# Output rows of a fused scan and feed-forward kernel placed in buffers that an earlier phase has left

## Chip, cores, metric

One Trainium2 chip, one core. The metric is the device time of one execution in microseconds; lower is better. A version is timed in rounds beside the kernel before on the same chip.

In the lines of the profile PE is TensorE, DVE VectorE, ACT ScalarE, POOL GpSimd, and SPq the queue of SyncE (SP), from which most transfers are issued. A line gives start and duration in microseconds, the engine, the line of the kernel (L622), output and inputs; `x3` means three instructions merged. A bracket at the end is the idle time before and what the profile thinks ended it. "Granted clock" is the share of TensorE's full clock that it got; a half-clock window is a stretch at 0.50.

## The reference, cut to what matters

```python
B, H, S, D = 4, 8, 768, 48
for t in range(S):                      # complex decay a_n, |a_n| <= 0.999
    S_re, S_im = a_n[t] * (S_re, S_im)  # complex product
    S_re += outer(k[t], v[t])
    y[t] = q[t] @ S_re
x = y.transpose(0, 2, 1, 3).reshape(3072, 384)
ffn = (gelu(x @ w_gate) * (x @ w_val)) @ w_out
out = x + sigmoid(x @ w_res) * ffn      # (3072, 384) fp32
```

The scan is done in 12 chunks of 256 steps (`g`), grouped in units `u`: [0], [1,2], [3,4], [5,6], [7,8], [9,10], [11]. In one phase the kernel finishes the attention part of unit `u`, prepares the decays of unit `u+1` and writes the output rows of unit `u-1`. So "the third phase" writes the rows of unit 1 (`op_step(1, 0..3)`), and 128 tokens are one output row block, called a row here. The gelu stretch of a phase is where PE computes `gp` and `vp` (`x @ w_gate`, `x @ w_val`) and ACT the gelu.

## The kernel before: what the change and the argument touch

```python
sqp = ctx.enter_context(tc.tile_pool(name="sqp", bufs=2))   # has the tags "qk" and "atm"
ob  = ctx.enter_context(tc.tile_pool(name="ob", bufs=2))    # the output rows
...
TURN = 3            # chunks g < 3: q and k are turned by TensorE and copied to "qk";
                    # chunks g >= 3: turned by DMA transposes (QT, KT)
...
# attention, chunks 1 and 2 only
qk = sqp.tile([128, 1024], BF, tag="qk", name="qk")
nc.scalar.copy(out=qk[0:DD, 0:512], in_=tp[0:DD, 0:512])
nc.vector.tensor_copy(out=qk[0:DD, 512:1024], in_=tp[0:DD, 512:1024])
...
def op_step(u, jj):
    h2 = T["h2", u]
    ps = psM.tile([128, DM], FP, tag="mm", padded_shape=[128, 512], name="op")
    for ffi in range(KF):
        nc.tensor.matmul(out=ps, lhsT=h2[:, ffi, jj * 128:(jj + 1) * 128], rhs=wo[:, ffi, :],
                         start=(ffi == 0), stop=(ffi == KF - 1))
    ot = ob.tile([128, DM], FP, tag="ot", name="ot")
    nc.vector.scalar_tensor_tensor(out=ot, in0=T["sg", u][:, jj], scalar=1.0, in1=ps, op0=OP.add, op1=OP.mult)
    t0 = (CHUNK[UNITS[u][0] + jj // C] * C + jj % C) * 128
    ...
    nc.sync.dma_start(out=out[t0:t0 + 128, :], in_=ot)
...
# in the same queue (SP): loads of q, k, a_re, a_im, and the transposes
T["turn"] = nc.sync.dma_start_transpose(out=tt, in_=pads[nm, g % 2])
...
# second gelu stretch: one chunk's loads go between the two chunks' transposes
if u == 1:
    steps[4:4] = [call(late, "turn", call(load_a, g)) for g in range(8, 9)]
```

Tiles of one tag share the pool's buffers in turn; a tile that gets a buffer waits for whatever last read it. For an output row that is the store of the row that had the buffer before.

## Time and profile before

| | before |
|---|---|
| median of 3 runs (range) | 289.26 us (288.54 to 289.46) |
| the profiled run | 291.91 us, span 290.1 |
| PE, DVE, ACT busy | 84%, 74%, 68% |
| DMA queue of SP | 67.7% of 16 engines |
| waits of a row for a store | 1 of 24, 2.97 us |

The profile is of a run 2.7 us longer than the median, though it still counts as fast. The lines of the profile that count are shown in the prediction.

### The profile page before, as it was taken

The page shows a single profiled execution, that of the slowest core. Times are in us where ns is not written, and L with a number is a line of the kernel's source. Part 1 is how long each engine was busy: PE and PEld are TensorE (multiplying, and loading weights), DVE is VectorE, ACT ScalarE, POOL GpSimd, SP SyncE. Part 2 cuts the span into 40 slices and gives each one's busy share as a digit, 9 for nine tenths or more (in the row PEclk, how much of TensorE's full clock was granted, in tenths as well). Part 3 has the DMA queues.
Part 4 walks back from the last instruction along what each step waited for, and adds up shares of the span by engine and source line. Part 5 has one row for each costly group of instructions (what it writes and reads, how often), then busy time and mean ns, then how long its engine had stood idle before and what let it go on. Part 6 is the DMA issues. An engine that isn't in the chain of part 4 may idle for free.

```text
span 290.1 us, 5128 instructions
## 1 busy us (share of the span) xinstructions
PE 244.3 (84%) x1834; PEld 146.3 (50%) x1848; DVE 214.6 (74%) x376; ACT 198.6 (68%) x336; POOL 93.3 (32%) x141
## 2 busy tenths in 40 slices
PE   0444958979789979979699999989999998999994
PEld 0122536855444545534356554556545665456782
DVE  0679996993999667878396998869977677564553
ACT  4877997688894799855479975778565646455250
POOL 4021841130245405465304393124911242100220
PEclk9999768997999999999799999999999999999998
DMA  8999999899999999959999979999599566910631
GB/s 147 187 174 187 170 199 198 145 188 201 158 206 200 171 203 178 176 127 139 185 209 165 131 114 186 207 174 79 74 213 205 104 56 129 185 23 21 144 54 55
DMA packets 176001, 44.01 MB, mean 152 GB/s; under 512 B 165092, under 2 KB 175976, under 8 KB 175976
## 3 DMA queue, kind: packets, MB, share of 16 engines
q1 hardware_dynamic: 140744, 33.05, 67.7%
q0 software_dynamic: 35232, 10.64, 35.7%
q8 instruction: 14, 0.23, 0.3%
q14 instruction: 11, 0.09, 0.1%
HBM read 31.33 MB, written 9.08 MB: 139 GB/s over the span
## 4 chain that ended last, share of the span: by engine, by line
PE 60%; ACT 14%; DVE 10%; DMA 9%; issue 4%; SPq 2%; DVEq 0%; ACTq 0%
PE vp L599 14%; PE gp L595 13%; PE op L619 11%; PE csl L272 6%; DMA KT<-padK 3%; ACT L639 3%; PE cst L291 3%; PE rp L611 3%; DMA ar<-in_a_re_dram 3%; PE at L446 2%; ACT CS L144 2%; SPq L172 2%; PE dk L488 1%; DMA k<-in_k_dram 1%; ACT ar L144 1%
## 5 line engine op out<-in xcount | busy, mean ns | idle before, releaser
L144 ACT ACTIVATE h<-gp 128x512 bf16<-128x512 f32 (+1 forms) x84 | 44.5, 535 | 41.5 <-PE gp L595 41.2
L602 DVE SCALAR_TENSOR_TENSOR h<-h,vp 128x512 bf16<-128x512 bf16 (+1 forms) x84 | 50.3, 606 | 20.6 <-PE vp L599 13.3
L595 PE MATMUL gp<-xT,wg 128*128 128x512 bf16 (+1 forms) x238 | 61.2, 352 | 4.4 <-DVE xT L586 2.0
L599 PE MATMUL vp<-xT,wv 128*128 128x512 bf16 (+1 forms) x252 | 62.3, 354 | 0.9 <-ACT xT L584 0.8
L619 PE MATMUL op<-wo,h 128*128 128x384 bf16 x288 | 50.7, 326 | 1.3 <-ACT xT L584 1.3
L599 PEld LDWEIGHTS <-wv 128*128 128x128 bf16 x252 | 24.9, 99 | 23.9 <-issue 2.2
L619 PEld LDWEIGHTS <-h 128*128 128x128 bf16 x288 | 27.3, 98 | 18.5 <-issue 2.3
L634 POOL DMA_DIRECT2D out_dram<-x x22 | 19.9, 953 | 46.5 <-DMA out_dram<-ot 45.1
L595 PEld LDWEIGHTS <-wg 128*128 128x128 bf16 x252 | 23.7, 99 | 21.3 <-issue 4.5
L316 POOL DMA_DIRECT2D m<-d x32 | 22.5, 709 | 36.4 <-DMA d<-Ei 15.4
L449 DVE TENSOR_TENSOR atm<-at,mask 128x512 bf16<-128x512 f32 x36 | 24.6, 683 | 9.0 <-PE at L446 9.0
L639 ACT ACT_TABLE_LOAD x21 | 26.9, 1283 | 1.1 <-PEq L844 0.7
L178 POOL DMA_DIRECT2D v<-in_v_dram x24 | 21.6, 906 | 17.6 <-DMA ai<-in_a_im_dram 12.3
L201 POOL COPY landed<-k 1x1 f32<-1x1 f32 x9 | 2.7, 296 | 65.2 <-DMA k<-in_k_dram 65.2
L272 PE MATMUL csl<-lm,lt0a 128*128 128x384 f32 x24 | 12.1, 589 | 11.6 <-ACT lm L144 11.6
L622 DVE SCALAR_TENSOR_TENSOR ot<-sg,op 128x384 f32<-128x384 f32 x24 | 13.1, 547 | 11.4 <-PE op L619 6.9
L446 PE MATMUL at<-QT,KT 96*128 96x128 bf16 x144 | 14.4, 220 | 4.5 <-DMA KT<-padK 4.0
L291 PE MATMUL cst<-ai,ut0b 128*128 128x384 f32 x40 | 17.3, 523 | 0.6 <-DVE ot L622 0.4
L144 ACT ACTIVATE CS<-ai,hpi 128x768 bf16<-128x768 f32 x12 | 11.2, 935 | 8.7 <-DVE ai L301 8.7
L144 ACT ACTIVATE ar<-ar 128x768 f32<-128x768 f32 x20 | 16.9, 853 | 0.1
L501 ACT CAST x<-y 128x384 bf16<-128x384 f32 x22 | 10.5, 477 | 9.3 <-PE y L498 8.8
L235 DVE CUSTOM_DVE_ANT_0 lm<-lm,sq 128x768 f32<-128x768 f32 x12 | 11.4, 949 | 7.3 <-ACT sq L231 7.3
(113 smaller groups left out, 458.2 us busy)
## 6 DMA issues: line engine op xcount, KB each, us to landing
ar<-in_a_re_dram SPq DMA_DIRECT2D x24, 192.0 KB, 5.6
ai<-in_a_im_dram SPq DMA_DIRECT2D x24, 192.0 KB, 4.4
q<-in_q_dram SPq DMA_DIRECT2D x24, 192.0 KB, 4.1
k<-in_k_dram SPq DMA_DIRECT2D x24, 192.0 KB, 5.1
out_dram<-ot SPq DMA_DIRECT2D x24, 192.0 KB, 2.8
out_dram<-x POOLq DMA_DIRECT2D x22, 192.0 KB, 4.8
v<-in_v_dram POOLq DMA_DIRECT2D x24, 96.0 KB, 5.0
wg<-in_moe_w_gate_dram POOLq DMA_DIRECT2D x4, 288.0 KB, 7.7
```

Of the source, the lines that this page charges most:

```text
L144: return tab(nc.scalar.activation(**kw))
L178: held(nc.gpsimd.dma_start(out=t[:, c], in_=rows(v, g, c)), after)
L272: nc.tensor.matmul(out=cs, lhsT=lmat[c], rhs=T["lm", g][:, sl], start=True, stop=True)
L291: nc.tensor.matmul(out=cs, lhsT=tmat[c if s == 0 else 1], rhs=th[:, sl], start=True, stop=(s == 0 or c == 0))
L316: T["turned"] = nc.gpsimd.dma_start(out=m[u * D:(u + 1) * D].rearrange("p r h -> p (r h)"), in_=md.rearrange("r (h d) -> d (r h)", h=H))
L446: nc.tensor.matmul(out=at[:, j], lhsT=T["KT", g][0:DD, x0 + j], rhs=T["QT", g][0:DD, x0 + j], start=True, stop=True)
L449: nc.vector.tensor_tensor(out=atm, in0=at, in1=mask4, op=OP.mult)
L595: nc.tensor.matmul(out=gp, lhsT=wg[:, fi, ffi * 128:(ffi + 1) * 128], rhs=xT[:, fi, :], start=(fi == 0), stop=(fi == KD - 1))
L599: nc.tensor.matmul(out=vp, lhsT=wv[:, fi, ffi * 128:(ffi + 1) * 128], rhs=xT[:, fi, :], start=(fi == 0), stop=(fi == KD - 1))
L602: T["gmul"] = nc.vector.scalar_tensor_tensor(out=h2[:, ffi, :], in0=h2[:, ffi, :], scalar=0.5, in1=vp, op0=OP.mult, op1=OP.mult)
L619: nc.tensor.matmul(out=ps, lhsT=h2[:, ffi, jj * 128:(jj + 1) * 128], rhs=wo[:, ffi, :], start=(ffi == 0), stop=(ffi == KF - 1))
L639: tab(nc.scalar.preload_act_table_set(nm))
```

## The change

Its intent: give the output rows more buffers without more memory. After chunk 2 the two `qk` buffers are never used again, so rows with odd number, from the third phase on, go there.

```diff
-        ot = ob.tile([128, DM], FP, tag="ot", name="ot")
+        if u > 0 and jj % 2:
+            ot = sqp.tile([128, 1024], BF, tag="qk", name="ot2").bitcast(FP)[:, 0:DM]
+        else:
+            ot = ob.tile([128, DM], FP, tag="ot", name="ot")
```

## The prediction

> **What bounds the kernel now.** I read the page first, then the waits of the whole run and those of VectorE (DVE) alone, then the chain that ended last, then timelines of the stretch that the waits pointed to, and last that stretch's DMA share.
>
> The page says that no engine is full on average: PE 84%, DVE 74%, ACT 68%. The chain says what sets the end after the first half: from 150 us on it is nearly all matmuls, and between 150 and 264 us PE is busy 110.2 of 114 us (the windows view). So time saved before 150 us arrives at the end unless DMA holds it up; store waits after 150 us would have to show in the waits view first.
>
> The change can only act where an output row `ot` waits for a buffer. DVE's waits, longest first in total (us in total, times, longest), show one such wait:
>
> ```profile
> DVE h L602 <- PE vp L599: 13.3, 27, 0.7
> DVE atm L449 <- PE at L446: 9.0, 8, 2.5
> ...
> DVE ot L622 <- DMA out_dram<-ot: 3.0, 1, 3.0
> ```
>
> One of the 24 rows waits for a store to land, for 3.0 us. A second view agrees: of the 20 separate semaphore instructions that the sequencer runs ahead of the `ot` line, the median takes 21 ns and the longest 2095 ns. The DVE timeline shows where (start, duration, what, [idle before]):
>
> ```profile
> 117.83 0.54 DVE L622 SCALAR_TENSOR_TENSOR ot<-sg,op 128x384 f32<-128x384 f32 x1
> ...
> 121.62 0.55 DVE L296 TENSOR_TENSOR lm<-cst,lm 128x384 f32<-128x384 f32 x1
> 125.14 0.55 DVE L622 SCALAR_TENSOR_TENSOR ot<-sg,op 128x384 f32<-128x384 f32 x1 [2.97 <-DMA out_dram<-ot]
> 125.61 0.55 DVE L301 TENSOR_SCALAR ai<-lm 128x768 int32<-128x768 int32 x1
> 126.08 0.35 DVE L586 COPY xT<-tpx 128x384 bf16<-128x384 bf16 x1
> 126.35 0.94 DVE L381 TENSOR_TENSOR padQ<-CS,q 128x1536 bf16<-128x1536 bf16 x1
> ```
>
> This is the third row of the third phase. The first row was computed at 113.17; its store left eight microseconds later, because the sync queue (SP) was still issuing loads:
>
> ```profile
> 118.45 3.04 SPq L164 DMA_DIRECT2D ai<-in_a_im_dram  x2
> 121.59 4.47 SPq L626 DMA_DIRECT2D out_dram<-ot  x3
> 127.36 3.22 SPq L385 DMA_TRANSPOSE QT<-padQ  x1
> 130.67 0.53 SPq L626 DMA_DIRECT2D out_dram<-ot  x1
> 131.25 3.83 SPq L385 DMA_TRANSPOSE KT<-padK  x1
> ```
>
> The chain that ended last goes through this very wait (start, us, what):
>
> ```profile
> 121.59 3.46 DMA out_dram<-ot
> ...
> 125.14 0.55 DVE ot L622
> 125.70 0.48 DVE ai L301
> 126.18 0.02 issue
> 126.20 1.67 ACT CS L144 x2
> 127.87 0.02 issue
> 127.89 1.28 ACT L639
> ...
> 131.25 10.00 DMA KT<-padK
> ```
>
> So the reader should see a store issued late, not a slow store, and a DVE that stands in order behind it with ready work (`ai`, `xT`, `padQ`).
>
> **What the Trainium skill says.** (1) "TensorE: Matmul & The Clock Gate", section "Architectural detail", calls ACT and DVE strict FIFO. The trace agrees: L301 had its input at 122.17 and started at 125.61, after `ot`. (2) "Perfetto Trace Analysis", section "DMA Instruction — HWDGE", says that the queue's row starts when its semaphores are satisfied and leaves out the data movement. The trace agrees: the store's row starts at 121.59 and DVE is released at 125.05, 3.46 us on. (3) "DMA: Bandwidth & Descriptors", section "Issuing engines are not separate DMA queues": all DMAs share 16 engines. It matters for whether transposes moved forward would meet loads; see below. (4) The clock-gate page, section "What's actually happening": the clock falls to half after an idle window of about 3.4 us, the window running freely. The trace has such a fall: after PE's wait for `KT` the granted clock was 0.50 in 142 to 144 us and 0.77 in 144 to 146.
>
> **The change, part by part.** It adds and removes no instruction. Rows with odd number, in the third and later output phases, take the `qk` buffers: 4+4+4+4+4+2 = 22 rows lie there, so 11 move and 13 stay. A row is 384 fp32 = 1536 bytes per partition and the `qk` buffer 2048, so it fits and costs no memory. The `ot` instruction stays 128x384 fp32 from PSUM, 0.55 us. The last matmul reading `qk` started at 72.7 us (view of that tile); the first row put there belongs at about 117.8, so the new buffers bring no wait of their own.
>
> In the third phase rows 0 to 3 now have four buffers: row 2 takes the one last used by the second phase's second row, stored long ago. Its other inputs: the matmuls of row 2 start at 119.50 and last 2.11, end 121.61; DVE is free at 122.17. So row 2 starts near 122.17 and not 125.14: **2.97 us**, all of that idle stretch.
>
> Does it reach the end? Step by step after it:
> - DVE: L301 at 122.6, `xT` at 123.1 (its transpose ends 122.93), `padQ` at 123.4, done 124.3, `padK` 125.2. Row 3 follows at about 125.1; its matmuls started 122.77 and end 124.88, just in time. Full 2.97 kept.
> - ACT: idle 3.66 us before `CS` for L301. It starts 2.97 earlier, as do the table load (127.89 to 124.9) and the first gelu (129.18 to 126.2).
> - PE: its first `gp` waits 1.60 us for `xT`. That wait goes; PE is then free at 124.9, gains 1.6, fills its four PSUM buffers, and waits for the gelu. From the gelu on (129.83 resumption becomes 126.9) it is 2.97 earlier, so the end of `rp` moves from 138.73 to 135.8.
> - SP: loads end at 121.5 as before; the third store leaves near 123, `QT` at 124.4 instead of 127.36, row 3's store after it, `KT` at 128.3 instead of 131.25. With 3.83 of issue and 6.17 to landing, as now, `KT` lands at 138.3 instead of 141.25.
> - So PE's wait for `KT` stays 2.56 us, between 135.8 and 138.3, and everything behind it is PE work shifted by 2.97.
>
> Is there room in DMA? The windows view, one us each (last two columns: share of 16 engines, GB/s), says yes:
>
> ```profile
> 124.00:125.00 1.00, 0.89 (x6) 0.40 (x5) 0.00 (x0) 0.00 (x0) 0.98 (x3) 1.00 0.83 219
> 125.00:126.00 1.00, 0.00 (x0) 0.00 (x0) 0.86 (x2) 0.00 (x0) 0.00 (x0) 1.00 0.22 33
> ...
> 128.00:129.00 1.00, 0.91 (x5) 0.38 (x4) 1.00 (x3) 1.00 (x1) 1.00 (x2) 1.00 0.00 0
> ```
>
> The loads have drained by 125; the engines then stand nearly empty until the transposes start. A `QT` issued at 124.4 meets only the last of the loads; I charge an estimated 0.2 us for it (a third of the 0.6 us between 124.4 and 125). Sum: 289.26 - 2.97 + 0.2 = **286.5 us**.
>
> Later phases: no other row waits for a store, and their rows 0 and 2 lie 6 to 9 us apart with the first store issued within 0.6 us (the fourth phase: row 0 at 159.18, store 159.75, row 2 at 167.70). Gain there: nil.
>
> **Rivals.**
> - *The wait is replaced.* If `KT` comes no earlier, because the transposes are paced by the loads before them, PE waits for it longer and nothing is gained: about 289. For it: `KT` already makes PE wait 2.56 us, and the second unit's `QT` issue took 6.51 us, so transposes do queue up. Against: the DMA share of 0.00 at 128 to 129. I give it one in ten, and half-way cases (287.5 to 288.5) the same.
> - *The clock.* The shift moves PE's idle stretch against the freely running clock window. The present fall costs, as an estimate from the granted clocks, 2 x (0.12 + 0.50 + 0.23) = 1.7 us. If the new run escapes it, 285; if it meets a second one, 288. Neither has evidence; one in eight each.
> - *The order changes.* Buffer availability could enter how the instruction streams are put in order. Against: in the third, fourth and fifth phases alike DVE runs the last L296, row 2, then L301, though only the third phase has the wait; the order does not look shaped by it. If it changes anyway, either direction by up to 2%.
> - *The wait was hidden anyway.* Then 289. Against: DVE, ACT (3.66) and PE (1.60) idle together there.
>
> **Range and chances.** The three runs before spread 0.9 us. Full gain, 286.3 to 286.7, is the likeliest; a partly lost gain stretches the range up more than a lucky clock stretches it down: 285.3 to 288.3. Over 2% faster means below 283.5, twice the one wait there is; only a new order or clock could do that: 4%. Over 2% slower: 3%. Within: 93%.
>
> **What would show it right or wrong.** Right: no DVE wait for `out_dram<-ot`; row 2 near 122.2 and L301 right behind it; `QT` issue at 124.4 and `KT` landing near 138.3; the stretch after it the same as before but about 2.8 to 3.0 us earlier; `ot` still 0.55 us. Wrong: PE's wait for `KT` grows from 2.56 towards 5; or the granted clock differs at 138 to 146; or DVE's sequence differs; or the wait reappears at another row.

## The result

| | before | changed |
|---|---|---|
| median (range), same rounds | 288.9 us (287.73 to 289.46, 4 runs) | 285.74 us (284.71 to 289.11, 4 runs) |
| ratio | | 0.9884, interval 0.9834 to 0.9934 |
| profiled span | 290.1 | 282.9 |

A ratio here is the mean time of one kernel's fast runs over that of the other's fast runs in the same rounds, so it is not quite the ratio of the medians. One of the four runs of the changed kernel (289.11) counts as slow and is left out of it. Executions over 1.5% slower than the fastest of the same kernel are left out of the means. The predicted 286.5 lies 0.8 us from the median.

The order of the instructions on every engine was compared: it is the same in both kernels. So no gain comes from a new order; what can differ is where rows lie, how long instructions wait, and what follows.

The DVE timeline of the changed kernel (L625 is the row, L622 before), the counterpart of the stretch shown in the prediction:

```profile
117.67 0.55 DVE L625 SCALAR_TENSOR_TENSOR ot<-sg,op 128x384 f32<-128x384 f32 x1
...
121.46 0.55 DVE L296 TENSOR_TENSOR lm<-cst,lm 128x384 f32<-128x384 f32 x1
121.93 0.54 DVE L625 SCALAR_TENSOR_TENSOR ot<-sg,op 128x384 f32<-128x384 f32 x1
122.39 0.55 DVE L301 TENSOR_SCALAR ai<-lm 128x768 int32<-128x768 int32 x1
122.86 0.35 DVE L586 COPY xT<-tpx 128x384 bf16<-128x384 bf16 x1
123.12 0.95 DVE L381 TENSOR_TENSOR padQ<-CS,q 128x1536 bf16<-128x1536 bf16 x1
```

There is no bracket behind row 2 any more, and the row takes the same 0.54 us. The queue of SP in the changed kernel:

```profile
117.07 3.24 SPq L164 DMA_DIRECT2D ai<-in_a_im_dram  x2
120.41 2.42 SPq L629 DMA_DIRECT2D out_dram<-ot  x3
124.14 1.80 SPq L385 DMA_TRANSPOSE QT<-padQ  x1
126.03 1.08 SPq L629 DMA_DIRECT2D out_dram<-ot  x1
127.16 3.98 SPq L385 DMA_TRANSPOSE KT<-padK  x1
```

The stores still leave only when the loads are out (120.41), 7 us after row 0 was computed. What changed is that nobody waits for them. `QT` leaves 3.2 us earlier than before.

The spans of the two profiles differ by 7.2 us, more than twice what the times differ by. Two things lie behind that, both in the stretch after row 2. PE's waits between 126 and 150 us, before and then changed:

```profile
PE at L446 <- DMA KT<-padK: 2.6, 1, 2.6
PE gp L595 <- DVE xT L586: 1.6, 1, 1.6
```

```profile
PE dk L488 <- DVE Gb L411: 0.2, 1, 0.2
```

The wait for `KT`, which I had expected to stay, is gone. And so is the half-clock window that followed it. The windows view (after the busy times: clock granted, DMA share, GB/s), before, cut at the clock's own steps, and then changed:

```profile
138.09:141.50 3.41, 0.85 (x8) 0.40 (x7) 1.32 (x6) 2.27 (x5) 2.05 (x3) 1.00 1.36 199
141.50:144.91 3.41, 3.19 (x19) 1.81 (x18) 1.15 (x2) 0.60 (x1) 0.00 (x0) 0.50 1.32 178
```

```profile
137.00:146.00 9.00, 8.92 (x98) 5.58 (x98) 8.29 (x15) 7.22 (x15) 0.64 (x1) 1.00 1.33 204
```

The clock did not simply get better, though. The changed profile has a half-clock window of its own in the second phase, from 104.98 to 108.39 us, which the one before lacks. Of the later profiles below, all nine of edited or changed kernels that are of use have it there too, and not behind `KT`; the useful one of the kernel before (rerun_before2) again has it only behind `KT`. Row 0 of the third phase came at 112.5 to 114.6 us with the earlier window (turn_first, with another order of loads, apart) and at 113.2 and 113.6 without it.

One profile each cannot tell which of this belongs to the change and which to the run. The experiments had to.

### The profile page after: what moved, and what is told of

It is laid out like the page before. It is cut to its first block, busy times and chain, and to the rows that moved or that the text cites. A ratio compares the mean times of both kernels' runs of the same rounds, so it can differ in the third digit from the quotient of the medians.

```text
span 282.9 us, 5119 instructions
## 1 busy us (share of the span) xinstructions
PE 242.6 (86%) x1834; PEld 145.9 (52%) x1848; DVE 215.1 (76%) x376; ACT 198.8 (70%) x336; POOL 93.8 (33%) x141
## 4 chain that ended last, share of the span: by engine, by line
PE 66%; ACT 11%; DMA 7%; SPq 6%; issue 4%; DVE 3%; POOL 2%; ACTq 0%; DVEq 0%; POOLq 0%
PE op L619 14%; PE vp L599 14%; PE gp L595 14%; PE csl L272 6%; SPq L164 4%; PE cst L291 3%; PE rp L611 3%; PE at L446 2%; DMA ar<-in_a_re_dram 2%; ACT L642 2%; DMA d<-lm 2%; PE dk L488 2%; PE cst L293 2%; PE tpx L580 2%; DMA k<-in_k_dram 2%
## 5 line engine op out<-in xcount | busy, mean ns | idle before, releaser
L637 POOL DMA_DIRECT2D out_dram<-x x22 | 20.7, 988 | 42.0 <-DMA out_dram<-ot 37.5
L625 DVE SCALAR_TENSOR_TENSOR ot<-sg,op 128x384 f32<-128x384 f32 x24 | 13.2, 549 | 8.6 <-PE op L619 5.6
L501 ACT CAST x<-y 128x384 bf16<-128x384 f32 x22 | 10.5, 477 | 8.8 <-PE y L498 8.5
L144 ACT ACTIVATE sg<-rp 128x384 f32<-128x384 f32 x24 | 11.6, 491 | 6.5 <-PE rp L611 5.4
```

The costliest lines, as they stand in the source:

```text
L144: return tab(nc.scalar.activation(**kw))
L637: nc.gpsimd.dma_start(out=out[t0:t0 + 128, :], in_=x, accum_op=OP.add)
```

## The experiments

Theory: one wait, row 2 of the third phase for row 0's store, is all that the change removes, and its 3 us reach the end. Rivals: the later phases' buffers carry some of it; it is chance; the buffers' place and not their number matters; the store is slow, not late. Twelve kernels ran, four on one chip each. Single runs scatter more on these chips than the first three did: the kernel before ranged from 286.2 to 292.7 within one call.

### Is it chance? Both kernels again

No edit to either. rerun_before:

> The kernel before, unchanged, against itself. If the gain of the change is real and not drawn by chance: ratio 1.000 within 0.004. If run-to-run scatter alone makes 1% (rival), the ratio can be as far off as 0.99. Its second profile: DVE waits again 2 to 4 us for the store of row 0 at row 2 of the third phase; PE waits for KT about 2.6 us after that if this wait belongs to the kernel, anything from 0 to 3 us if it is a matter of the run.

rerun_after:

> The changed kernel again, for a second profile. My theory (one wait of 3.0 us removed and carried to the end): ratio 0.988 to 0.991, no DVE wait for a store in the third phase, and if my step on KT was right PE waits about 2.6 us for KT in the third gelu stretch; the first profile of the changed kernel showed no such wait. If it is absent again, the moved transposes land sooner than I reckoned, and the gain in the profile is above 3 us.

Measured (ratio to the kernel before, interval): rerun_before 1.0003 (0.9942 to 1.0063); rerun_after 0.9919 (0.9866 to 0.9972). The profiled run of rerun_before took 637 us, with PE busy for 602 of them, and says nothing about the kernel. The profile of rerun_after has neither the wait at row 2 nor a `KT` wait behind it. Later, on a third chip, both once more. rerun_before2:

> The kernel before against itself again, because its last profile was of a run of 635 us and is no use. Ratio 0.997 to 1.003. Profile: the wait of 2 to 3.5 us at row 2 of the third phase, and 1.5 to 3 us of PE wait for KT behind it, with a half-clock window after it if PE's wait is over 2 us.

rerun_after2:

> The changed kernel beside third_only3 on the same chip, to settle whether the third phase alone carries the gain. My theory: 0.988 to 0.993 and within 0.004 of third_only3. Profile: no store wait at row 2, a PE wait for KT behind it of 0 to 1.3 us, not the 2.56 of my prediction.

Measured: rerun_before2 1.0015 (0.9973 to 1.0057); rerun_after2 0.9918 (0.9885 to 0.9952). The profile of rerun_before2 fell in a slow run (295.7 us), so it only illustrates: 3.97 us at row 2, 3.6 for `KT`. The profile of rerun_after2 has no `KT` wait either, but a new one in its place (DVE, then PE):

```profile
139.49 0.16 DVE L361 TENSOR_TENSOR M<-m 96x8 f32<-96x8 f32 x1 [2.67 <-DMA m<-d]
```

```profile
140.97 0.38 PE L446 MATMUL at<-QT,KT 96*128 96x128 bf16 x4 [2.19 <-DVE atm L449]
```

A small transfer of decays, issued by POOL, came late in this run: POOL waited 6.3 us for the transfer that it depends on, against 2.2 in the first profile of the changed kernel. So what stands ready behind the removed wait varies by run: `KT` or this.

What follows: not chance. Three independent ratios, 0.9884, 0.9919 and 0.9918, agree that the change takes 0.8 to 1.2%, that is 2.3 to 3.4 us; the kernel against itself stays within 0.2%.

### The wait put back

```diff
+        held(<row>, T["st", u, jj - 2] if u == 1 and jj > 1 else None)   # rows 2, 3 of the third phase
-        nc.sync.dma_start(out=out[t0:t0 + 128, :], in_=ot)
+        T["st", u, jj] = nc.sync.dma_start(out=out[t0:t0 + 128, :], in_=ot)
```

(Shortened: `<row>` stands for the `scalar_tensor_tensor` of the row.) `held` makes an instruction wait for another's completion; the edit puts back row 3's wait for row 1 too. All new buffers stay.

> The changed kernel with all its buffers, but row 2 of the third phase made to wait for the store of row 0, as the old buffers made it. My theory: the whole gain is lost, ratio 0.998 to 1.002, and the profile shows the 3 us DVE wait at row 2. Rival (the gain comes from buffers elsewhere or from the layout): ratio stays 0.988 to 0.991.

Measured: 1.0063 (1.0007 to 1.0118). The gain is lost, and 0.6% more; for the excess I have no cause. The profile fell in a run at a granted clock of 0.841 (311.8 us) and cannot show the wait: with TensorE that slow, row 2 (128.20) waits for its own matmuls, and the store of row 0, issued at 122.75, had landed 4.0 us later, at 126.8.

```profile
128.20 0.55 DVE L625 SCALAR_TENSOR_TENSOR ot<-sg,op 128x384 f32<-128x384 f32 x1 [0.45 <-PE op L619]
```

What follows: with the wait back the new buffers are worth nothing, those of the later phases included. That rests on the times alone; the next experiments show the wait itself.

### The third phase alone, the later phases alone

```diff
-        if u > 0 and jj % 2:
+        if u == 1 and jj % 2:      # third_only
+        if u > 1 and jj % 2:       # later_only
```

third_only, which was run three times since the first did not decide:

> The new buffers in the third phase alone, the later phases as before. My theory: the whole gain, ratio 0.988 to 0.991, the same as the full change. Rival (later phases gain too): ratio 0.993 to 0.997.

> The new buffers in the third phase alone, once more, because the first time (ratio 0.9999, interval 0.9936 to 1.0063, single times 287.7 to 292.0) decided nothing. My theory: 0.988 to 0.992 as for the full change. Rival (the later phases' buffers carry the gain in unprofiled runs): 0.997 to 1.003 again.

> The new buffers in the third phase alone, third time (0.9999 and 0.9932 so far). My theory: 0.990 to 0.995, within 0.004 of rerun_after2. Rival (later buffers give part of the gain in runs that the profile does not show): 0.996 to 1.000 and at least 0.005 above rerun_after2.

later_only:

> The new buffers from the fourth phase on, the third as before. My theory: no gain, ratio 0.997 to 1.003, and the profile has the 3 us DVE wait in the third phase again, with a PE wait for KT behind it. Rival (later phases carry the gain): ratio 0.988 to 0.993.

Measured: third_only 0.9999 (0.9936 to 1.0063), 0.9932 (0.9895 to 0.9969), 0.9941 (0.9897 to 0.9984); later_only 1.0025 (0.9988 to 1.0062). The profile of later_only, whose third phase is as before, has the wait in a fast run:

```profile
122.66 0.55 DVE L296 TENSOR_TENSOR lm<-cst,lm 128x384 f32<-128x384 f32 x1
125.60 0.55 DVE L625 SCALAR_TENSOR_TENSOR ot<-sg,op 128x384 f32<-128x384 f32 x1 [2.39 <-DMA out_dram<-ot]
```

What follows: the later buffers alone gain nothing, as expected. The third phase alone gains in two runs of three, and less than the full change: 0.0080 and 0.0023 above it where both ran on the same chip. Over all runs third_only averages 0.9957 and the full change 0.9907, so on this count the third phase alone has a little under half of the gain; the first run, with single times from 287.7 to 292.0 (against 285.9 to 287.7 for the full change), makes part of the gap. My theory wanted the whole gain here, and the rival that the later buffers carry a part is not ruled out. later_only does not settle it, since it keeps the wait in the third phase; the later buffers may count only once that wait is gone and the fourth phase starts earlier.

There are traces of it. None of third_only's three profiles names a wait for a store, but in the fourth phase of third_only2 row 2 stood idle for 0.40 us, put down to a matmul whose result it does not read, 5.7 us after the store of row 0 had been issued. And in qk_pair, the next experiment, whose fourth phase has the old two buffers, row 2 does wait there (its row 0's store was issued at 159.30):

```profile
164.66 0.56 DVE L625 SCALAR_TENSOR_TENSOR ot<-sg,op 128x384 f32<-128x384 f32 x1 [1.00 <-DMA out_dram<-ot]
```

From row 0 of that phase to the end qk_pair took no longer than the others (131.1 us, see below), so what such a wait costs is not shown. Whether the later buffers are worth some tenths of a per cent stays open.

### The number of buffers, or which?

```diff
-        if u > 0 and jj % 2:
+        if u == 1:                 # qk_pair: all four rows of the third phase in the two qk buffers
```

> All four rows of the third phase in the two qk buffers, so again two buffers for four rows, though the new ones; other phases in their old pair. My theory (the number of buffers counts, not which): row 2 waits again about 3 us for row 0's store, ratio 0.997 to 1.004. Rival (the old pair is bad by its place or by the second phase's use of it): ratio 0.988 to 0.993.

Measured: 1.0002 (0.9959 to 1.0045). DVE in that profile, and the landing of the one store issued between 120 and 122 us (at 121.22; view of the tile):

```profile
121.16 0.55 DVE L296 TENSOR_TENSOR lm<-cst,lm 128x384 f32<-128x384 f32 x1
124.25 0.56 DVE L625 SCALAR_TENSOR_TENSOR ot<-sg,op 128x384 f32<-128x384 f32 x1 [2.55 <-PE op L619]
```

```profile
DMA to landing us min/median/max: 2.9/2.9/2.9
```

The bracket names PE, and it is wrong. The 12 matmuls of this row are all in the trace and ended at 121.0; those that end near 124.25 are row 3's (122.14 to 124.26), which row 2 does not read. The store left at 121.22 and landed 2.9 later, at 124.1; DVE started at 124.25. Two buffers for four rows bring the wait back wherever they lie: it is the number.

### Late, or slow?

```diff
-        nc.sync.dma_start(out=out[t0:t0 + 128, :], in_=ot)
+        (nc.scalar if u == 1 and jj < 2 else nc.sync).dma_start(out=out[t0:t0 + 128, :], in_=ot)
```

On the kernel before: two buffers, but the first two stores of the third phase are issued by ACT, not behind the loads.

> The old two buffers; the first two stores of the third phase are issued by ACT instead of the queue that is still issuing loads. My theory says the store was late, not slow: issued at about 114 and not 121.6, it lands near 118, before row 2 asks at 122.2, so the 3 us wait goes without any new buffer and the ratio is 0.989 to 0.994 (ACT pays under 1 us of issue per store in a busy stretch). Rival (stores land late because the DMA engines are full of loads): row 2 still waits 2 us or more, ratio 0.997 or above.

Measured: 0.9977 (0.9937 to 1.0017). The wait at row 2 is gone, without a new buffer, but ACT pays for it:

```profile
116.70 0.37 ACTq L626 DMA_DIRECT2D out_dram<-ot  x1
117.12 0.49 ACT L144 ACTIVATE Ei<-csl 128x384 f32<-128x384 f32 x1 [3.63 <-DMA ar<-in_a_re_dram]
```

Row 0 was ready at 114.11. But in the program the store also waits for a semaphore on which an earlier load (`ar`) counts, so ACT stood until that load had landed, with its own work behind it. ACT's exponentials, the table load and all behind them came 3 us late, and row 2 ran at 124.58. The store was late, not slow: issued at 116.70 instead of 121.59 it landed 4.9 us later, at 121.6, before row 2 had asked at 122.17 in the kernel before. Amid the loads it took 1.4 us longer than the 3.46 there, so the rival has a little to it. That it was issued no earlier than 116.70 I had not foreseen, and the ratio missed my range and is what the rival expected: only the trace speaks for "late". Nor is the edit as clean as it looks, for the order of a few instructions moved with it (DVE runs L301 before row 1, not after); that the wait only moved from DVE to ACT is the likely reading of the time.

### A version that might beat both

The changed kernel still waits 1.4 us for `KT` in the second phase (at 103.66) and runs a half-clock window right behind. Four loads stand ahead of that transpose in the queue. The edit puts them behind it; only SP's order changes.

```diff
-            steps[4:4] = [call(late, "turn", call(load_a, g)) for g in range(8, 9)]
+            steps += [call(late, "turn", call(load_a, g)) for g in range(8, 9)]
```

> The changed kernel, with four loads of a later step queued behind the second pair of transposes of the second phase instead of ahead of it. The changed kernel still waits 1.4 us for KT there (at 103.7) and runs a half-clock window right after. If that KT is late because its issue stands behind the loads, it lands about 5 us earlier, the wait goes, and with it perhaps the half-clock window: ratio to the kernel before 0.980 to 0.987. Rival (the loads are then late themselves, for the ACT work at 112): 0.990 or above.

Measured: 1.0124 (1.0082 to 1.0165). The rival was right. The second pair of transposes went out 5 us earlier, and PE's wait for `KT` in the second phase is gone; but the loads came late for ACT:

```profile
103.45 0.84 ACT L217 ACTIVATE lm<-ar 128x768 f32<-128x768 f32 x1 [3.34 <-DMA ar<-in_a_re_dram]
106.01 0.84 ACT L231 ACTIVATE sq<-ai 128x768 f32<-128x768 f32 x1 [1.72 <-DMA ai<-in_a_im_dram]
```

PE then waited 6.5 us in one piece for the copy of `x` (L501) that ACT reached too late. No version that ran is faster than the changed kernel.

### One interval over all profiles

The time from row 0 of the third phase to row 0 of the fourth, both read as start of the DVE row in the timelines, isolates the stretch. Profiles of fast runs only:

| two buffers in the third phase | us | more buffers in the third phase | us |
|---|---|---|---|
| before | 113.17 to 159.18: 46.0 | changed | 112.82 to 151.96: 39.1 |
| later_only | 114.02 to 157.04: 43.0 | rerun_after | 114.27 to 153.44: 39.2 |
| qk_pair | 112.52 to 155.06: 42.5 | rerun_after2 | 113.85 to 155.37: 41.5 |
| act_store (wait moved to ACT) | 113.56 to 156.90: 43.3 | third_only, 2, 3 | 40.5, 39.1, 40.1 |

turn_first, a fast run with more buffers but another order of loads, has 40.0 (118.67 to 158.67). From row 0 of the fourth phase to the end it is 130.9 to 132.5 us in all of them. So the profiles differ mostly within this one interval. Its excess over 39.1 is the row's wait plus what stood ready behind: 2.97 for the row, 2.56 for `KT` and a half-clock window in the first profile; 2.39 and 1.6 in later_only, with no half-clock window.

## Why the prediction was right

- **The wait of row 2 in the third phase: right.** It is in every fast profile with two buffers there and the stores in SP's queue (2.97, 2.39, 2.55 in qk_pair), and in none with more. wait_back, later_only and qk_pair have it or its like and no gain.
- **The store is late and not slow: right**, by the trace of act_store, not by its time.
- **DVE's sequence after it: right to 0.3 us.** Row 2 at 121.93 (reckoned 122.17), L301 at 122.39 (122.6), `padQ` 123.12 (123.4). Row 0 itself was 0.35 earlier in this run. The end of `rp`, reckoned at 135.8, came at 135.9.
- **`QT` at 124.4: right** (124.14). **`KT` issued at 128.3 and landed 10.0 later: wrong in the second half.** It left at 127.16, 1.1 sooner than reckoned, mainly because `QT`'s issue took 1.80 us and not 3.22, and was in use at 135.73 without a wait, so it needed at most 8.6 from the start of its issue. PE's wait of 2.56 us for it, which I carried over from one profile, is absent in all three profiles of the full change and 1.2 and 0.8 in two of third_only's three. The first profile was of a run 2.7 us over the median, and its `KT` wait was probably part of that: with two buffers, later_only had 1.6 and qk_pair 1.0. Why transposes land sooner in one run than in another, no run here settles.
- **The clock as a rival at one in eight: it happened in the first pair of profiles.** A half-clock window behind `KT` in the third phase is only in the first profile before, and in the slow one. By the interval above it explains part of the 7.2 us between the first two profiles. For its part in the 2.3 to 3.4 between the times there is no evidence: unprofiled runs show only a mean clock.
- **Nil in later phases: open.** It was read from one profile. later_only supports it; the gap between third_only and the full change, and the 1.00 us of qk_pair in the fourth phase, speak against it. Nor do all rows 0 and 2 lie 6 to 9 us apart: in the seventh phase it is 4.6 (266.52 and 271.13), where the store of row 0 landed in 1.9.
- **The size: 2.77 forecast, 2.3 to 3.4 measured** in three sets of rounds. The profiles give somewhat more, 3.9 us (mean 43.9 for before, later_only and qk_pair, against 39.9 for the six of the right column), from few and scattered samples. That the sum came out so near is in part luck: it kept a `KT` wait that went, it took the row's wait from the longest of the three fast profiles, and it counted nothing for the later phases. The 0.2 us charged for `QT` was not seen: its issue got shorter.

## What to carry to other kernels

Look for the instruction that waits for a store to land, and then for when the store was issued: here a transfer of 3.5 us stood 7.9 us behind loads in an in-order queue, and more buffers cost less than a new order of the queue. The two attempts at reordering (a store on another engine, transposes ahead of loads) removed the wait that they aimed at and lost about as much or more at an engine whose work then stood in line. And treat the waits behind the one you remove as samples: read them in several profiles before you put them in a sum.

## What the Trainium skill lacked or had wrong

- "DMA: Bandwidth & Descriptors", section "Issuing engines are not separate DMA queues", says that issuing from several engines saves only the sequencer's time, "usually small relative to the DMA itself". Here it was not small in sum: in the kernel before, the 16 loads from 102.37 to 121.49 us took 1.2 us of SP each (their landing took 4.1 to 5.6, median of each kind over the run), and a row's store that itself needs 3.46 us stood 7.9 us behind them.
- No page has a figure for what the wait of a transfer costs the compute engine that issues it. In act_store ACT idled 3.63 us around its own store, most of it on the semaphore of an earlier load.
- "TensorE: Matmul & The Clock Gate", section "What's actually happening", ties the half clock to an idle window of about 3.4 us. The window length agrees (3.41), but the window need not be idle, as the prediction's reading of it had it: with PE busy 0.85 of 3.41 us (138.09 to 141.50, before) and even 1.42 of 3.41 (101.57 to 104.98, changed) the next one ran at 0.50.
- No page says how much the landing of a DMA transpose varies: the same `KT` in the third phase took 10.0 us from the start of its issue in one run and at most 8.6 in another.
